# A gated feed-forward kernel: the first stage loads part of x by transposing DMA and its weights through ScalarE's queue

## The chip, the cores and the metric

The kernel runs on one core of one Trainium2 chip. The metric is the device time of one execution in microseconds; the time before is the median of three runs, 558.75 us (558.51 to 558.77). A core has TensorE (PE, matrix multiplies), VectorE (DVE), ScalarE (ACT), GpSimd (POOL) and SyncE (SP, which issues DMAs). Each engine works through its own instructions in order; ScalarE can issue DMAs too, in its own queue. They meet at semaphores.

## What is computed

```
B, S, Dm, Df = 1, 2048, 1024, 3584          # all tensors bf16
g = x @ w_gate                              # [2048, 3584]
u = x @ w_up                                # [2048, 3584]
h = gelu(g) * u                             # tanh form of gelu
out = h @ w_down                            # [2048, 1024]
```

## The kernel before, in words

The 2048 rows of x are done in two passes of 1024 rows, each as two halves of 512 (`xT[0]` and `xT[1]`, held transposed: 128 rows of the contraction on the partitions, eight blocks `ko`, 512 columns). A pass has 14 units (`unit`, L193), one for each 256 columns of `w_gate` and `w_up`, and then `down` (L351) for the product with `w_down`.

A unit computes its 2x2 blocks with seven products in place of eight (Strassen's scheme, in Winograd's form). That needs sums of blocks of x (`t1` to `t4`, L136) and of the weights (`s1` to `s4`, L151), made in fp32r. The x sums are made by VectorE once for a pass. The weight sums are made for each unit: by VectorE for unit 1 of pass 0 and unit 0 of pass 1, by GpSimd for all others (`make_s(ahead, pool)`, L510, one unit ahead). Casts to fp32r (`tb`, `sa`) and copies out of the matmul banks (`snap`) are ScalarE's.

`down` uses the same scheme. For it the raw blocks of `w_down` have to be summed too. In pass 0 GpSimd does that beside the units: `keep(j)` (L258) makes three sums of block j into a tile `m` with one buffer, and `store_made(j)` (L269) writes them to a DRAM tile `td`, from where `load12` (L276) and `load4` fetch them in both passes. Blocks 11, 12 and 13 come in the last unit of pass 0, the last two into spare weight buffers (`w`). SyncE issues all of these DMAs in one written order, among them `fetch12` (L316), which loads the raw halves of `w_down` that `down`'s first product needs (tile `raw`, L319).

The first stage (L417 to L493) stands ahead of the units of pass 0. It does unit 0 without the scheme, in plain bf16 products (`plain`, L451), since sums aren't there yet: for the first 512 rows into banks 0 to 3, then for the second 512 rows into banks 4 to 7. Its weights `wf` come in pieces of `ko`. `w` there (`load_w(1)`, L449) is unit 1's weight tile, w1 below; w2 is the tile after it. x is loaded as it lies in memory (`load_x`, L422, four tiles of 128 rows and 1024 columns) and transposed by TensorE against an identity into a bank, eight 128x128 blocks a tile, and copied from there into `xT` by VectorE or ScalarE (`turn`, L431). Between these stand five warm-up matmuls on zeros, the sums t1, s1, t2, s2, t3, s3, and `finish` (L466): a gelu by ScalarE and a product by VectorE for each of two column blocks.

In the first unit of the schemes (u = 1) `aside(-1)` issues the load of w2 on ScalarE's queue, kept in program order behind the copies `p1` of the first product; `aside(0)` makes s4 and t4 on VectorE. After that `prepare` (L506) has GpSimd make the sums of w2: that is its first work apart from the identity. In pass 0's `down` the x of pass 1 is loaded by transposing DMAs (L553), issued by SyncE between other loads.

The order of SyncE, VectorE, GpSimd and TensorE is the program's (`manual_schedule`), in the first stage ScalarE's too.

Of the kernel before, what the change touches and what calls it, by code (L numbers as in the profile page):

```python
# [10 lines left out]
def kernel(  # L11
# [23 lines left out]
    nc = tc.nc  # L35
    ENG = mybir.EngineType
    ORDER = {ENG.SP, ENG.DVE, ENG.Pool, ENG.PE}
    P = nc.NUM_PARTITIONS
    bf16 = mybir.dt.bfloat16
# [6 lines left out]
    x2 = x.flatten_outer_dims()  # L46
    out2 = out.flatten_outer_dims()
    S, Dm = x2.shape
    Df = w_gate.shape[1]

    NKB = Dm // P
    KH = NKB // 2
    NFB = Df // P
    NJ = NFB // 2
    N = 512
    NS = N // P
# [14 lines left out]
    wpool = ctx.enter_context(tc.tile_pool(name="w", bufs=3))  # L71
# [4 lines left out]
    def new_x():  # L76
        return [xpool.tile([P, NKB, N], bf16, name=f"xT{c}") for c in range(2)]
# [4 lines left out]
    def slot(shape, dtype, name):  # L82
        return kpool.tile(shape, dtype, name=name, tag="k")


    bank = [psum.tile([P, N], f32, name=f"bank{i}") for i in range(8)]
# [23 lines left out]
    def matmul(ps, lhs, rhs, start, stop):  # L110
        nc.tensor.matmul(  # L111
            ps, lhsT=lhs, rhs=rhs, start=start, stop=stop, skip_group_check=True
        )
# [3 lines left out]
    def load_w(u, queue=nc.sync):  # L117
        f0 = u * 2 * P
        w = wpool.tile([P, 2, NKB, 2 * P], bf16, name="w")
        for i, src in enumerate((w_gate, w_up)):  # L120
            got = queue.dma_start(
                out=w[:, i],
                in_=src[:, f0 : f0 + 2 * P].rearrange("(ko ki) f -> ki ko f", ki=P),
            )
            if queue is not nc.sync:
                tc.keep_in_program_order(got)
        return w
# [23 lines left out]
    def sums_s(w, eng):  # L151
        GU = range(2)
        sh = [P, KH, P]
        a11, a21 = [[w[:, i, :KH, h : h + P] for i in GU] for h in (0, P)]
        a12, a22 = [[w[:, i, KH:, h : h + P] for i in GU] for h in (0, P)]
        return Sums(
            how={
                "s1": lambda q: [new(eng, a21[i], a22[i], ADD, "s1", sh) for i in GU],
                "s2": lambda q: [new(eng, q["s1"][i], a11[i], SUB, "s2", sh) for i in GU],
                "s3": lambda q: [new(eng, a11[i], a21[i], SUB, "s3", sh) for i in GU],  # L160
                "s4": lambda q: [new(eng, a12[i], q["s2"][i], SUB, "s4", sh) for i in GU],
                "sa": lambda q: [cast(a22[i], "sa", sh) for i in GU],
            }
        )
# [6 lines left out]
    def make_s(w, eng):  # L171
        s = sums_s(w, eng)
        s.make("s1", "s2", "s3", "sa", "s4")
        return s
# [244 lines left out]
    ident = xpool.tile([P, P], bf16, name="ident")  # L419
    make_identity(nc, ident)  # L420

    def load_x(c):  # L422
        t = []
        for i in range(NS):
            xn = slot([P, Dm], bf16, "xn")
            r0 = c * N + i * P
            nc.sync.dma_start(out=xn, in_=x2[r0 : r0 + P, :])
            t.append(xn)
        return t

    def turn(xT, xn, c, i, copy):  # L431
        tp = bank[4 + i].bitcast(bf16).rearrange("p (k r) -> p k r", k=NKB)
        for ko in range(NKB):
            nc.tensor.transpose(tp[:, ko, :], xn[i][:, ko * P : (ko + 1) * P], ident)
        copy(out=xT[c][:, :, i * P : (i + 1) * P], in_=tp)

    xT = new_x()
    xn0 = load_x(0)
    wf = wpool.tile([P, 2, NKB, 2 * P], bf16, name="w")
    for k0, k1 in ((0, 2), (2, 5), (5, NKB)):  # L440
        for i, src in enumerate((w_gate, w_up)):
            nc.sync.dma_start(
                out=wf[:, i, k0:k1],
                in_=src[k0 * P : k1 * P, 0 : 2 * P].rearrange(
                    "(ko ki) f -> ki ko f", ki=P
                ),
            )
    xn1 = load_x(1)
    w = load_w(1)  # L449

    def plain(ps, c, kos, parts=1):  # L451
        n = N // parts
        for k in range(kos.start, kos.stop, 2):
            for part in range(parts):
                cols = slice(part * n, (part + 1) * n)
                for p, (j, i) in zip(ps, [(j, i) for j in range(2) for i in range(2)]):
                    for ko in (k, k + 1):
                        matmul(
                            p[:, cols],
                            wf[:, i, ko, j * P : (j + 1) * P],  # L460
                            xT[c][:, ko, cols],
                            ko == 0 and part == 0,
                            ko == NKB - 1,
                        )

    def finish(ps, c):  # L466
        for j in range(2):
            times(j, c, gelu(ps[2 * j]), ps[2 * j + 1])

    on_dve, on_act = nc.vector.tensor_copy, nc.scalar.copy  # L470
    s, t = sums_s(w, dve), sums_t(xT)
    with tc.manual_schedule(engines={ENG.Activation}):
        for _ in range(NWARM):
            nc.tensor.matmul(bank[3], lhsT=warm[:, :P], rhs=warm, start=True, stop=True)
        for i in range(NS):
            turn(xT, xn0, 0, i, on_act if i == 1 else on_dve)
        plain(bank[0:4], 0, range(0, 2), parts=2)
        plain(bank[0:4], 0, range(2, 4))
        for i in range(2):
            turn(xT, xn1, 1, i, on_act if i % 2 else on_dve)  # L480
        plain(bank[0:4], 0, range(4, 6))
        for i in range(2, NS):
            turn(xT, xn1, 1, i, on_act if i % 2 else on_dve)
        plain(bank[0:4], 0, range(6, NKB))
        t.make("t1")
        s.make("s1")
        finish(bank[0:4], 0)
        t.make("t2")
        s.make("s2")
        t.make("t3", "tb")  # L490
        s.make("s3", "sa")
        plain(bank[4:8], 1, range(NKB))
        finish(bank[4:8], 1)  # L493

    def making(u):
        if u < 2 or u >= NU:
            return []
        return list(range(u - 2, NJ if u == NU - 1 else u - 1))
# [3 lines left out]
    for ip in range(NPASS):  # L502
        for u in range(1 if ip == 0 else 0, NU):
            js = making(u) if ip == 0 else []

            def prepare():  # L506
                nonlocal ahead
                nxt["w"], nxt["s"] = ahead, None
                if u + 1 < NU:
                    nxt["s"] = make_s(ahead, pool)  # L510
                if u + 2 < NU:
                    ahead = load_w(u + 2)
                if ip == 0:
                    fetch_wd(making(u + 1))
                    for j in making(u - 1):
                        store_made(j)
                for j in js:
                    keep(j, j != js[0])

            def aside(part):  # L520
                nonlocal ahead
                if ahead is None:
                    ahead = load_w(2, nc.scalar)
                if part == 0 and "s4" not in s:
                    s.make("s4")
                    t.make("t4")

            def ahead_of_p4():
                if u + 1 < NU:
                    nxt["p1"] = first_product(even if u % 2 else odd, xT, nxt["w"])  # L530

            e = odd if u % 2 else even
            p1 = nxt.pop("p1", None) or first_product(e, xT, w)
            unit(u, (e, cc, dd), xT, w, s, t, p1, prepare, aside, ahead_of_p4, ip == 0 and u == 1)
            if u + 1 < NU:
                w, s = nxt["w"], nxt["s"]

        last = ip == NPASS - 1
        got, nxt = {}, {}

        def more(step):

            nonlocal ahead
            if last:
                return
            if step == 0:
                xT[:] = new_x()
                for j in making(NU - 1):
                    store_made(j)
            if step >= 16 and step % 2 == 0 and step // 2 - 8 < len(moves):  # L550
                c, ko = moves[step // 2 - 8]
                r0 = (2 * (ip + 1) + c) * N
                nc.sync.dma_start_transpose(  # L553
                    out=xT[c][:, ko, :], in_=x2[r0 : r0 + N, ko * P : (ko + 1) * P]
                )
            if step == 50:
                got["w"], ahead = load_w(0), load_w(1)
            if step == 58:
                got["s"] = make_s(got["w"], dve)
            if step == 62:  # L560
                got["t"] = make_t(xT)

        down(ip, even + cc, dd + odd, last, more)
        even, odd, cc, dd = odd, even, dd, cc
        if not last:
            w, t, s = got["w"], got["t"], got["s"]
# [29 lines left out]
```

## Time and profile before

| what | value |
|---|---|
| median of the runs | 558.75 us (558.51 to 558.77, 3 runs) |
| the profiled execution, its own time | 558.77 us |
| span of the profiled execution (first to last instruction) | 557.0 us |
| TensorE busy | 539.8 us (97%) |
| VectorE busy | 326.2 us (59%) |
| ScalarE busy | 245.4 us (44%) |
| GpSimd busy | 281.3 us (51%) |
| granted TensorE clock, mean | 0.991 |
| DMA | 93.29 MB, 167 GB/s mean |
| first real work of TensorE / begin of unit 1 on TensorE | 3.40 us / 23.16 us |
| first sum of GpSimd for w2 begins / ends | 32.46 us / 35.13 us |

The first stage in the trace, in order of time:

| us | what |
|---|---|
| 0.74 to 2.55 | SyncE issues the four tiles of the first 512 rows of x |
| 2.59 to 5.65 | the six pieces of `wf` |
| 5.69 to 7.60 | the four tiles of the second 512 rows |
| 7.64 to 9.36 | w1, gate and up half |
| 3.40 to 6.42 | TensorE transposes the first rows |
| 6.42 to 10.11 | `plain`, first rows, ko 0 to 3 |
| 10.44 to 14.74 | the rest of it up to ko 5, the transposes of the second rows between |
| 14.74 to 23.16 | `plain`, first rows, ko 6 and 7, then all of the second rows |
| 15.99 to 38 | VectorE works without a break: t1, s1, finish 0, t2, s2, t3, s3, finish 1, then unit 1's sums with s4 (30.42) and t4 (31.62 to 34.11) between |
| 25.31 and 25.77 | ScalarE's queue issues w2, gate and up half |

How to read the profile lines further on: times are microseconds from the span's start. A line of a timeline gives start, duration from the first to the last instruction of the group, engine, source line, operation, output and input by tile name, how many, and in brackets how long the engine was idle before and what released it. SPq and ACTq are the queues in which SyncE and ScalarE issue DMAs; the duration of such a line is that of issuing, not of the transfer. "DMA to landing" is the time from the begin of the issue to the last byte's arrival.

### The profile page before, as it was taken

The numbers are of one execution on the slowest core, as the hardware profiler recorded it, in microseconds if no ns is written. First come the engines' busy times: TensorE is split into PE (matmuls) and PEld (weight loads), VectorE is DVE, ScalarE is ACT, GpSimd is POOL, SyncE is SP. The second block draws the span as 40 slices with busy tenths as digits, with TensorE's granted clock in tenths as the row PEclk, the third lists the DMA queues.
The fourth block names the chain that finished last, engine by engine and source line by source line (L and its number), as shares of the span: only waits on it lengthen the run. The fifth ranks groups of instructions, "written<-read, shape, count | busy, mean of one in ns | idle before, by whom it ended". The sixth has DMA issues, their size and how long they took to land.

```text
span 557.0 us, 7388 instructions
## 1 busy us (share of the span) xinstructions
PE 539.8 (97%) x2437; PEld 380.3 (68%) x2437; DVE 326.2 (59%) x492; ACT 245.4 (44%) x429; POOL 281.3 (51%) x248
## 2 busy tenths in 40 slices
PE   8999999999999939999999999999999999999997
PEld 4577776676677514788877777776766776478886
DVE  2994455545554893469675544555455557856730
ACT  2655554555555201035535555555554552104541
POOL 0069999999999630000049766677777700000000
PEclk9999999999999969999999999999999999999999
DMA  9384676766624579998926233322222049553751
GB/s 277 90 237 114 189 195 186 215 188 182 172 95 171 188 281 324 306 261 231 333 76 154 80 106 106 88 75 76 76 78 75 1 129 381 188 185 118 228 188 58
DMA packets 104359, 93.29 MB, mean 167 GB/s; under 512 B 12929, under 2 KB 88705, under 8 KB 104321
## 3 DMA queue, kind: packets, MB, share of 16 engines
q1 hardware_dynamic: 102240, 91.77, 55.7%
q10 hardware_dynamic: 2080, 1.05, 0.7%
q8 instruction: 20, 0.33, 0.3%
q14 instruction: 19, 0.15, 0.1%
HBM read 75.50 MB, written 15.20 MB: 163 GB/s over the span
## 4 chain that ended last, share of the span: by engine, by line
PE 59%; DMA 4%; POOL 2%; issue 1%; SPq 1%; ACT 0%; POOLq 0%
PE bank L111 59%; DMA raw<-in_w_down_dram 3%; POOL w L93 1%; DMA td<-w 1%; POOL m L93 1%; DMA td<-m 1%; SPq L319 1%; SPq L553 0%; ACT st L398 0%; SPq L280 0%; POOLq L93 0%
## 5 line engine op out<-in xcount | busy, mean ns | idle before, releaser
L93 POOL TENSOR_TENSOR s<-w 128x512 fp32r<-128x512 bf16 x100 | 118.5, 1206 | 157.8 <-DVE t L90 86.8
L111 PE MATMUL bank<-t,s 128*128 128x512 f32 x648 | 157.0, 398 | 0.0
L111 PEld LDWEIGHTS bank<-t,s 128*128 128x128 f32 x648 | 121.8, 188 | 27.7
L107 ACT COPY p<-bank 128x512 f32<-128x512 f32 x124 | 71.3, 589 | 114.3 <-PE bank L111 114.3
L111 PE MATMUL bank<-xT,w 128*128 128x512 bf16 (+1 forms) x504 | 116.6, 377 | 0.0
L90 DVE TENSOR_TENSOR hT<-g,bank 128x512 bf16<-128x512 f32 x112 | 76.7, 687 | 55.0 <-ACT g L178 46.7
L90 DVE TENSOR_TENSOR sum<-bank,p 128x512 f32<-128x512 f32 x54 | 37.3, 691 | 88.4 <-PE bank L111 80.8
L111 PEld LDWEIGHTS <-w 128*128 128x128 bf16 x504 | 45.0, 98 | 58.7 <-issue 13.5
L178 ACT ACTIVATE g<-sum 128x512 f32<-128x512 f32 x81 | 51.3, 633 | 56.6 <-DVE sum L90 55.1
L111 PE MATMUL bank<-raw,hT 128*128 128x512 bf16 x224 | 51.7, 392 | 11.7 <-DMA raw<-in_w_down_dram 11.7
L111 PE MATMUL bank<-q 128*128 128x512 f32 x240 | 59.0, 389 | 0.0
L111 PE MATMUL bank<-t,sa 128*128 128x512 f32 x216 | 58.7, 413 | 0.0
L93 POOL TENSOR_TENSOR s<-w,s 128x512 fp32r<-128x512 bf16 x50 | 57.7, 1177 | 0.0
L93 POOL TENSOR_TENSOR s<-s,w 128x512 fp32r<-128x512 f32 x50 | 57.2, 1166 | 0.0
L111 PE MATMUL bank<-tb,s 128*128 128x512 f32 x216 | 53.3, 389 | 0.0
L111 PEld LDWEIGHTS bank<-q 128*128 128x128 f32 x240 | 45.1, 188 | 9.3
L111 PEld LDWEIGHTS <-hT 128*128 128x128 bf16 x224 | 22.4, 101 | 40.7 <-issue 16.6
L111 PEld LDWEIGHTS bank<-t,sa 128*128 128x128 f32 x216 | 40.7, 188 | 10.6
L111 PEld LDWEIGHTS bank<-tb,s 128*128 128x128 f32 x216 | 40.6, 188 | 8.4
L107 ACT COPY u<-bank 128x512 f32<-128x512 f32 x62 | 35.8, 589 | 23.7 <-PE bank L111 23.3
L102 ACT CAST tb<-raw 128x512 fp32r<-128x512 bf16 x28 | 17.2, 627 | 63.3 <-PE bank L111 27.0
L90 DVE TENSOR_TENSOR q<-hT 128x512 fp32r<-128x512 bf16 x56 | 41.6, 742 | 3.4 <-PE bank L111 3.4
(43 smaller groups left out, 466.9 us busy)
## 6 DMA issues: line engine op xcount, KB each, us to landing
raw<-in_w_down_dram SPq DMA_DIRECT2D x80, 256.0 KB, 3.5
q<-td SPq DMA_DIRECT2D x60, 256.0 KB, 5.0
w<-in_w_gate_dram SPq DMA_DIRECT2D x26, 512.0 KB, 4.2
w<-in_w_up_dram SPq DMA_DIRECT2D x26, 512.0 KB, 5.5
td<-m SPq DMA_DIRECT2D x12, 768.0 KB, 4.5
w<-td SPq DMA_DIRECT2D x6, 1024.0 KB, 8.2
out_dram<-st SPq DMA_DIRECT2D x32, 128.0 KB, 1.7
xn<-in_x_dram SPq DMA_DIRECT2D x8, 256.0 KB, 4.3
```

What stands on the lines that cost most here:

```text
L90: nc.vector.tensor_tensor(out=out, in0=a, in1=b, op=op)
L93: nc.gpsimd.tensor_tensor(out=out, in0=a, in1=b, op=op)
L102: nc.scalar.copy(out=t, in_=src)
L107: nc.scalar.copy(out=t, in_=ps)
L111: nc.tensor.matmul(ps, lhsT=lhs, rhs=rhs, start=start, stop=stop, skip_group_check=True)
L178: nc.scalar.activation(g, src, ACT.Gelu_apprx_tanh)
L319: nc.sync.dma_start(out=rl, in_=wdn[:, kh, j : j + 2, :N])
```

## The change

Only the first stage differs.

- The first 512 rows: columns 0 to 511 (ko 0 to 3) are loaded by four transposing DMAs of 512 rows and 128 columns on SyncE's queue, straight into `xT[0]`. Columns 512 to 1023 are still loaded as they lie (four tiles of 128 x 512) and turned by TensorE, four blocks a tile, into ko 4 to 7.
- The second 512 rows: all eight `ko` by transposing DMAs on SyncE's queue. TensorE and the copying engines have no work on them.
- `wf` (in pieces of ko 0-1, 2-3 and 4-7), the four half-width tiles of x and w1 are issued on ScalarE's queue, in program order.
- TensorE's order: warm-ups, ko 0, ko 1, two tiles turned, ko 2, two tiles turned, ko 3, then ko 4 to 7 in pairs, then the second rows.
- VectorE's order: t1, finish 0, s1, s2, t2, t3, s3, where it was t1, s1, finish 0, t2, s2, t3, s3.
- In `down` the transposing load moves into a helper, with the same instruction.

```diff
-    def load_x(c):
+    def load_x(c, queue):
...
-            xn = slot([P, Dm], bf16, "xn")
+            xn = slot([P, KH * P], bf16, "xn")
...
-            nc.sync.dma_start(out=xn, in_=x2[r0 : r0 + P, :])
+            got = queue.dma_start(out=xn, in_=x2[r0 : r0 + P, KH * P :])
+            tc.keep_in_program_order(got)
...
-        for ko in range(NKB):
+        for ko in range(KH):
             nc.tensor.transpose(tp[:, ko, :], xn[i][:, ko * P : (ko + 1) * P], ident)
-        copy(out=xT[c][:, :, i * P : (i + 1) * P], in_=tp)
+        copy(out=xT[c][:, KH:, i * P : (i + 1) * P], in_=tp[:, :KH])
+
+    def transposing(xT, c, ko, r0):
+        nc.sync.dma_start_transpose(
+            out=xT[c][:, ko, :], in_=x2[r0 : r0 + N, ko * P : (ko + 1) * P]
+        )
...
-    for k0, k1 in ((0, 2), (2, 5), (5, NKB)):
+    for ko in range(KH):
+        transposing(xT, 0, ko, 0)
+    load_wf(nc.scalar, 0, 2)
+    load_wf(nc.scalar, 2, 4)
+    xn0 = load_x(0, nc.scalar)
+    load_wf(nc.scalar, 4, NKB)
+    for ko in range(NKB):
+        transposing(xT, 1, ko, N)
+    w = load_w(1, nc.scalar)
...
-        for i in range(NS):
-            turn(xT, xn0, 0, i, on_act if i == 1 else on_dve)
-        plain(bank[0:4], 0, range(0, 2), parts=2)
-        plain(bank[0:4], 0, range(2, 4))
+        plain(bank[0:4], 0, range(0, 1))
+        plain(bank[0:4], 0, range(1, 2))
         for i in range(2):
-            turn(xT, xn1, 1, i, on_act if i % 2 else on_dve)
-        plain(bank[0:4], 0, range(4, 6))
+            turn(xT, xn0, 0, i, on_act if i % 2 else on_dve)
+        plain(bank[0:4], 0, range(2, 3))
         for i in range(2, NS):
-            turn(xT, xn1, 1, i, on_act if i % 2 else on_dve)
-        plain(bank[0:4], 0, range(6, NKB))
+            turn(xT, xn0, 0, i, on_act if i % 2 else on_dve)
+        plain(bank[0:4], 0, range(3, 4))
+        plain(bank[0:4], 0, range(4, NKB))
         t.make("t1")
-        s.make("s1")
         finish(bank[0:4], 0)
-        t.make("t2")
-        s.make("s2")
-        t.make("t3", "tb")
+        s.make("s1", "s2")
+        t.make("t2", "t3", "tb")
         s.make("s3", "sa")
         plain(bank[4:8], 1, range(NKB))
         finish(bank[4:8], 1)
```

`load_wf(queue, k0, k1)` issues the gate and the up piece of `wf` on the given queue; the loop that it replaces issued the same on SyncE's.

## The prediction

> **What bounds the kernel now.** I read the page's busy rows first, then the chain of waits, then GpSimd's and TensorE's timelines, then the first 36 us engine by engine. The busy rows of the page (tenths of 40 slices, 13.9 us each):
>
> ```profile
> PE   8999999999999939999999999999999999999997
> POOL 0069999999999630000049766677777700000000
> PEclk9999999999999969999999999999999999999999
> ```
>
> TensorE (PE) looks like the bound everywhere, but slice 14 has a hole (a 3, with the granted clock down), and GpSimd (POOL) is full from slice 3 up to just before that hole. The chain of waits says what filled it (start, duration, what):
>
> ```profile
> 181.66 4.45 issue
> ...
> 196.43 1.49 POOL w L93
> ...
> 199.50 4.32 DMA td<-w
> ...
> 204.92 2.39 SPq L319
> ...
> 224.37 329.45 PE bank L111 x1464
> ```
>
> Followed back, the end of the kernel hangs on GpSimd's last down-weight sum (199.50). SyncE's queue holds the store of those sums behind them, and behind that store it holds the reloads at L319 that feed the first down product. So TensorE waited here (start, duration, group, idle before it):
>
> ```profile
> 204.57 6.01 PE L111 MATMUL bank<-raw,hT 128*128 128x512 bf16 x16 [10.36 <-DMA raw<-in_w_down_dram]
> ```
>
> 10.36 us of TensorE's time in pass 0 are slack: if TensorE alone comes earlier or some microseconds later there, nothing at the end moves. What moves the end is when GpSimd begins, as its timeline shows:
>
> ```profile
> 32.46 3.79 POOL L93 TENSOR_TENSOR s<-w 128x512 fp32r<-128x512 bf16 x2 [31.16 <-DMA w<-in_w_gate_dram]
> 36.20 2.30 POOL L93 TENSOR_TENSOR s<-s,w 128x512 fp32r<-128x512 f32 x2
> ...
> 179.24 2.43 POOL L93 TENSOR_TENSOR m<-raw,m 128x512 fp32r<-128x512 bf16 x2
> 186.12 1.16 POOL L93 TENSOR_TENSOR m<-raw 128x512 fp32r<-128x512 bf16 x1 [4.46 <-issue]
> ```
>
> From 36.20 to 181.67 it has no gap at all; the one gap, 4.46 us, is the store of the single buffer m. So whatever shifts the first pair (32.46) shifts the kernel's end by as much. That pair takes 3.79 us where later pairs take 2.3: its first sum runs 2.67 us, to 35.13. VectorE's (DVE) timeline gives the reason:
>
> ```profile
> 30.42 1.28 DVE L90 TENSOR_TENSOR s<-w,s 128x512 fp32r<-128x512 bf16 x2
> 31.62 2.49 DVE L90 TENSOR_TENSOR t<-xT,t 128x512 fp32r<-128x512 bf16 x4
> 34.03 0.68 DVE L90 TENSOR_TENSOR hT<-g,bank 128x512 bf16<-128x512 f32 x1
> ```
>
> The four t4 sums end at 34.11, GpSimd's first 1.02 us later. At the start of pass 1 it is the same: VectorE's t sums end at 289.22, GpSimd's first, begun at 286.28, ends at 290.24, again 1.02 later. GpSimd stands still while VectorE runs back-to-back sums on two SBUF operands. So GpSimd's first sum ends at the later of (landing of w2's gate half plus about 1.1) and (end of t4 plus 1.02); the second sum needs the up half, landed by 34.21, where it could start at 35.09: 0.88 us to spare.
>
> **The change, part by part.** Call T0 to T11 the twelve transposing loads, all on SyncE: T0 to T3 fill xT0's ko 0 to 3, T4 to T11 xT1's ko 0 to 7.
>
> Removed on TensorE: 48 of 64 transposes. Eight take 0.45 us of weight loads (0.056 each at full rate): 48 are 2.7 us. Removed on VectorE and ScalarE: four of eight xT copies, the others halved; they had covers and cost no path. Bytes stay as they were: 8 x 256 KB of x and 2 MB of weights, 4.2 MB, which the first 16 us carried at 317 to 330 GB/s.
>
> Added on SyncE:
>
> ```profile
> L553 SPq DMA_TRANSPOSE xT<-in_x_dram x16: 1122/1138/2318, 212.0 to 253.0; - x16
> DMA to landing us min/median/max: 2.9/4.3/7.5
> ```
>
> Three of them back to back took 3.73 us with their gaps, so a pitch of 1.17 to 1.3 (the first of all took 2.32, with the queue full). I take 1.17: T_k is issued at 0.74 + 1.17k. T0 lands alone, 2.9 to 3.4 later: 4.0. In the loaded stretch I take 6.6, the landing of the second and third of pass 0, issued under a full queue (bounds 2.9 and 7.5): T7 lands at 0.74 + 8.2 + 6.6 = 15.5 (12 to 16.5). T11, when the rest is through, 4.3: 17.9 (16.5 to 21).
>
> A rule speaks against this: the Trainium skill, "VectorE: DVE Perf Modes", Rules for kernel authors, would give a 128x128 transpose to TensorE wherever PSUM will do as its target, and The three transpose paths puts it at 1309 ns by DMA against 390 by TensorE. One after the other 48 blocks would be an estimated 63 us by that page and the kernel some 45 us slower; the rows above, four blocks in 1.14 us of issue, overrule it.
>
> Moved to ScalarE (ACT): twelve loads (four of wf, four of half-width xn0, two of wf, two of w1), from 0.73 on. Issues on that queue cost 0.42 and 0.59 in the trace, so 6.4 us end it at best. But a queue with much outstanding holds its issuer: on SyncE w1's second half took 0.88 at 8.48, and the third and fourth of four such loads in a row 2.90 and 1.61 (260.9 to 265.5). I take 8.7 (6.4 to 9.5). Behind it wait ScalarE's table load (1.28, which ran at 0.73 in the idle start before) and its two xT copies, some 0.6 each (half of 1.01, plus its fixed part): done at 11.2 (9 to 12).
>
> TensorE then: ko 0 at 4.0, ko 1 with T1 (4.8) to 5.9, transposes of xn0 rows 0 and 1 (landed about 6.7), ko 2 (0.86), transposes 2 and 3 (about 8.1), ko 3 to 9.4; ko 4 to 7 wait for ScalarE's second copy, 11.2, and take 16 x 0.216 = 3.5: 14.7. Second rows 32 x 0.216 = 6.9: unit 1 begins at 21.6 against 23.16 (at 26.62 the first product with t follows 16 matmuls of 0.216). Without the hold it is 20.2, limited by transposes and landings; T11 needs no more than 17.9 + 0.9. The clock may stay halved for some microseconds more, since TensorE idles between warm-up and ko 0; the first eight matmuls would cost 1.7 us more, under the arrival of T2 and the copies.
>
> VectorE's order becomes t1, products of finish 0, s1, s2, t2, t3, s3, products of finish 1, s4, t4. t1 ends with T7: 15.5 + 0.7 = 16.2; the two products 17.4 (gelu is done by 15.0); w1, the last of 4.2 MB, has landed by then: 1.8 (first bytes) + 13.7 + 0.7. From s1 to finish 1 are 14 sums at 0.602: 8.4, so 25.8 against 28.03, 2.2 us earlier, and t4 ends at 31.9 (30.7 to 34). No stall of TensorE interferes: it supplies finish 1 by 22.
>
> GpSimd: w2 is issued behind unit 1's first copies, 2.15 after its begin: 23.75; its halves land 7.1 and 8.4 later as now: 30.9 and 32.6. That falls into the s4 and t4 run, so GpSimd's first sum ends at 31.9 + 1.02 = 32.9 against 35.13: **2.2 us earlier**, all of which reaches the end. Sum: profiled run 558.77 (span 557.0 and 1.77 around it; the median of the runs is 558.75) less 2.2 gives **556.6 us**. Its own range: t4 at 30.7 and unit 1 at 20.2 give 3.4 less, 555.3; t4 at 33 gives 557.6.
>
> **Rivals.** First, no gain: ScalarE's queue is served behind SyncE's. For it: w2, issued at 25.31, lies behind loads of SyncE, and from 25.4 to 28.4 only SyncE's queue moved bytes; the other came after 28.5. Then w1 lands after T11, near 19.6, s1 starts when it would have had to start anyway (18.40 and the 1.2 of the products now put ahead), and t4 ends at 34: 558.7. Against it: at a pitch of 1.17 the transposes leave the engines half free. The Trainium skill, "DMA: Bandwidth & Descriptors", Queues, rings and completion order, says that each DMA engine takes packets of the queues in turn; by that w1 would not wait and the estimate stays 556.6.
>
> Second, slower: both queues' issues pass one after the other, and the pitch of T grows. T11 at 0.74 + 11p + 4.3 decides when unit 1 begins (0.9 later). Up to T11 = 23.2, p = 1.65, GpSimd's 0.88 us of slack on the up half still covers it; above, each 0.1 of p costs 1.1 us. Twelve loads of 0.5 among twelve transposes of 1.2 make p = 1.7 (559.4); at 1.9 it is 561.5; at the 2.32 of the first one 566. For it: that 2.32, and landings of 6.6 to 7.5 under load. Against: three in a row under a busy queue kept 1.17 to 1.3.
>
> Third, more gain than I count: T7 lands by 13.5, ScalarE isn't held and unit 1 starts before 20: 555.
>
> **How the numbers follow.** Forecast (555.3 to 557.6) 0.58, more gain 0.04, no gain 0.20, slower 0.18. Within 0.2% of 558.75 is 557.6 to 559.9, about what a measurement of this kernel tells from no change. The no-gain case lies there; of the slower case 0.02 stays inside. Faster 0.62, same 0.22, slower 0.16. The range 555.2 to 559.8 leaves out some 0.04 below and 0.16 above.
>
> **What would show it.** GpSimd's first sum should end near 32.9 and right behind t4's end, its last near 197.3, and TensorE's wait before L319's data be about 9.7. The transposing loads should stand 1.17 to 1.3 apart and the twelfth land by 18; ScalarE's last first-stage issue should end near 8.7 and ko 4 start near 11. I am wrong if GpSimd pauses between 36 and 181, if the pitch is above 1.6, or if w1 lands after 19.

## The result and the profile after

| | before | after |
|---|---|---|
| median of the runs | 558.76 us (558.51 to 560.13, 4 runs) | 564.71 us (563.92 to 565.12, 4 runs) |
| span of the profiled execution | 557.0 us | 562.9 us |
| unit 1's first product with t on TensorE begins | 26.64 us | 33.98 us |
| t4 ends on VectorE | 34.11 us | 39.33 us |
| GpSimd's first sum ends / its third begins | 35.13 / 36.20 us | 41.08 / 42.82 us |
| GpSimd's last sum of pass 0 ends | 199.48 us | 205.77 us |

The changed kernel is slower: ratio 1.0100, 95% interval 1.0080 to 1.0119. The forecast was 556.6 us, faster, with a range of 555.2 to 559.8; the time lies 4.9 us above that range.

The end still hangs where it did. The chain of waits of the changed kernel (start, duration, what):

```profile
188.23 4.48 issue
...
204.27 1.50 POOL w L93
...
205.79 4.31 DMA td<-w
...
221.62 338.07 PE bank L111 x1504
```

GpSimd's (POOL) last down-weight sum, the store behind it, a reload of `raw`, and then TensorE to the end: the same links as before, each some 6 us later. (Before, TensorE waited once more, 0.23 us at 224.37, so its last piece is counted from there; the group that starts here at 221.62 started at 215.34.) TensorE's timeline, at the place where it had 10.36 us to spare:

```profile
210.84 5.30 PE L111 MATMUL bank<-raw,hT 128*128 128x512 bf16 x16 [9.29 <-DMA raw<-in_w_down_dram]
```

It still waits 9.29 us there. So TensorE's delay costs nothing at this place; what costs is that GpSimd began late. GpSimd's timeline, and VectorE's (DVE) beside it:

```profile
39.91 1.17 POOL L93 TENSOR_TENSOR s<-w 128x512 fp32r<-128x512 bf16 x1 [38.60 <-DMA w<-in_w_gate_dram]
41.71 1.16 POOL L93 TENSOR_TENSOR s<-w 128x512 fp32r<-128x512 bf16 x1 [0.64 <-DMA w<-in_w_up_dram]
42.82 2.30 POOL L93 TENSOR_TENSOR s<-s,w 128x512 fp32r<-128x512 f32 x2
```

```profile
36.84 2.49 DVE L90 TENSOR_TENSOR t<-xT,t 128x512 fp32r<-128x512 bf16 x4
39.25 0.68 DVE L90 TENSOR_TENSOR hT<-g,bank 128x512 bf16<-128x512 f32 x1
```

t4 is over before GpSimd's first sum begins, which now takes 1.17 us and not 2.67: nothing blocks it any more. It waits for w2, and w2 is issued by ScalarE behind unit 1's first product, 7.3 us later than before. The up half of w2 lands 7.45 us later (41.64 against 34.19); before, it had 0.88 us to spare, now the second sum waits for it, so the third sum begins 6.62 us later. From there to the end the kernel takes 0.7 us less than before, which no run explains; that leaves the 5.9 us of the span.

Why unit 1 is late is read in ScalarE's (ACT) timeline; ACTq lines are its DMA issues:

```profile
4.94 2.32 ACTq L427 DMA_DIRECT2D xn<-in_x_dram  x4
8.62 0.42 ACTq L445 DMA_DIRECT2D w<-in_w_gate_dram  x1
13.58 0.39 ACTq L445 DMA_DIRECT2D w<-in_w_up_dram  x1
14.01 0.52 ACTq L121 DMA_DIRECT2D w<-in_w_gate_dram  x1
14.57 0.65 ACTq L121 DMA_DIRECT2D w<-in_w_up_dram  x1
15.26 1.28 ACT L436 ACT_TABLE_LOAD   x1 [15.26 <-issue]
16.55 1.07 ACT L436 COPY xT<-bank 128x512 bf16<-128x512 bf16 x2
```

The issues take 0.35 to 0.65 us each, but there are holes of 2.20, 1.36 and 4.54 us before 4.94, 8.62 and 13.58. The program explains them, and the trace records which semaphore each DMA signals and which one its issue waits for: every DMA of both queues signals one of eight completion semaphores, given out in turn over both queues, and an issue waits until the DMA that had the same semaphore before has landed. The trace has these landings:

| issue on ScalarE's queue | at | the DMA that had its semaphore | landed |
|---|---|---|---|
| xn, first tile | 4.94 | T0, issued by SyncE at 0.74 | 4.92 |
| wf, ko 4 to 7, gate | 8.62 | xn, first tile | 8.60 |
| wf, ko 4 to 7, up | 13.58 | T6, issued by SyncE at 8.52 | 13.56 |
| w1, gate | 14.01 | T7, issued by SyncE at 9.83 | 13.99 |

So in three of the four, and in 6.7 of the 8.1 us of holes, ScalarE waits in its own issues for SyncE's transposing loads; the other one, at 8.62, waits for a plain load of its own queue. Behind these issues stand its table load and the two copies that ko 4 needs, and TensorE's timeline ends the story:

```profile
11.43 1.03 PE L111 MATMUL bank<-xT,w 128*128 128x512 bf16 x4
17.68 16.66 PE L111 MATMUL bank<-xT,w 128*128 128x512 bf16 x64 [5.21 <-ACT xT L436]
33.98 5.82 PE L111 MATMUL bank<-t,s 128*128 128x512 f32 x24
```

It stands still for 5.21 us, and then half its clock is gone. The stretches before and behind 17.6 us (the columns: stretch, its length, PE busy, granted clock, DMA share, GB/s):

```profile
12.50:17.60 5.10, 0.00 (x0) 0.87 1.01 201
17.60:23.10 5.50, 5.42 (x13) 0.50 0.80 166
```

13 matmuls in 5.42 us are 0.42 each, where 0.216 is the full rate. A last line asks for more than waits: what the DMA engines carried on both queues together from 1.8 to 11 us (the DMA view of that stretch, kernel after).

```profile
DMA packets 4977, 1.86 MB, mean 202 GB/s; under 512 B 3392, under 2 KB 4977, under 8 KB 4977
```

In the same 9.2 us the kernel before moved 2.92 MB at 318 GB/s, in 3164 packets. Now it is a third less, in more and smaller packets, with the engines shown as busy throughout (a DMA share of 0.99 to 1.26 from 3 to 13 us). Three suspects, then: the waits of one queue for the other, the transposing loads themselves, and the two queues side by side.

### The profile page after: what moved, and what is told of

It reads as the page before. It is cut to its first block, busy times and chain, and to the rows that moved or that the text cites. A ratio compares the mean times of both kernels' runs of the same rounds, so it can differ in the third digit from the quotient of the medians.

```text
span 562.9 us, 7271 instructions
## 1 busy us (share of the span) xinstructions
PE 540.0 (96%) x2381; PEld 377.2 (67%) x2381; DVE 324.1 (58%) x489; ACT 243.9 (43%) x428; POOL 279.5 (50%) x248
## 3 DMA queue, kind: packets, MB, share of 16 engines
q10 hardware_dynamic: 6880, 3.67, 2.8%
## 4 chain that ended last, share of the span: by engine, by line
PE 60%; DMA 3%; POOL 1%; issue 1%; ACT 0%; SPq 0%; POOLq 0%
PE bank L111 60%; DMA raw<-in_w_down_dram 2%; POOL w L93 1%; DMA td<-w 1%; POOL m L93 1%; DMA td<-m 1%; ACT st L398 0%; SPq L280 0%; POOLq L93 0%
## 5 line engine op out<-in xcount | busy, mean ns | idle before, releaser
L93 POOL TENSOR_TENSOR s<-w 128x512 fp32r<-128x512 bf16 x100 | 116.8, 1187 | 165.5 <-DVE t L90 86.4
L111 PE MATMUL bank<-xT,w 128*128 128x512 bf16 x496 | 121.0, 391 | 6.7 <-ACT xT L436 5.2
L111 PE MATMUL bank<-raw,hT 128*128 128x512 bf16 x224 | 50.9, 388 | 11.2 <-DMA raw<-in_w_down_dram 11.2
```

The source lines that it names most:

```text
L93: nc.gpsimd.tensor_tensor(out=out, in0=a, in1=b, op=op)
L111: nc.tensor.matmul(ps, lhsT=lhs, rhs=rhs, start=start, stop=stop, skip_group_check=True)
```

## The experiments

All in one table first. The ratio is to the kernel before, run on the same chip, with its 95% interval; e1 and e2 are single runs. The last three columns are of the profiled execution, whose own time can lie up to 1.7 us off the median (e3: 560.79, e10: 558.38): begin of unit 1's first product with t, begin of GpSimd's third sum, and how long after that the span ended.

| run | median us | ratio | t product | third sum | rest of the span |
|---|---|---|---|---|---|
| before | 558.76 | | 26.64 | 36.20 | 520.8 |
| after | 564.71 | 1.0080 to 1.0119 | 33.98 | 42.82 | 520.1 |
| e1 copies on VectorE | 563.78 | | 32.27 | 41.23 | 520.8 |
| e2 w1 on SyncE | 561.85 | | 31.15 | 39.89 | 520.1 |
| e3 fewer, larger loads | 562.32 | 1.0043 to 1.0081 | 29.69 | 38.59 | 520.4 |
| e4 w2 early | 562.07 | 1.0039 to 1.0079 | 26.74 | 29.20 | 530.8 |
| e5 straight loads | 560.37 | 1.0007 to 1.0046 | 29.43 | 38.34 | 520.2 |
| e6 filler matmuls | 562.37 | 1.0054 to 1.0099 | 31.27 | 40.05 | 520.1 |
| e7 second rows only | 566.59 | 1.0120 to 1.0156 | 28.35 | 34.51 | 530.0 |
| e8 weights on ScalarE | 563.17 | 1.0068 to 1.0098 | 31.52 | 41.09 | 520.7 |
| e9 gate half first | 560.53 | 1.0019 to 1.0043 | 27.35 | 38.25 | 520.8 |
| e10 gate half, w2 early | 556.70 | 0.9952 to 0.9975 | 27.96 | 35.92 | 520.5 |
| e11 straight, copies on VectorE | 557.28 | 0.9960 to 0.9984 | 26.52 | 35.28 | 520.1 |
| e12 mended change | 560.76 | 1.0022 to 1.0047 | 30.03 | 38.98 | 521.0 |

In twelve of fourteen rows the rest of the span is 520.1 to 521.0 us, while the third sum's begin moves over 7.5 us: the time of this kernel is read off the moment when GpSimd has its first pair of sums done. The two exceptions are taken up below.

**e1: are ScalarE's two copies the cause?** The changed kernel with all four copies on VectorE.

```diff
-            turn(xT, xn0, 0, i, on_act if i % 2 else on_dve)
+            turn(xT, xn0, 0, i, on_dve)
```

> The changed kernel with all four copies of turned x on VectorE instead of two on ScalarE. In the changed kernel the second rows' first matmul group (ko 4 on) began at 17.68, behind ScalarE's table load and two copies, which came behind its last DMA issue (15.22). Theory S (an issue on ScalarE's queue waits until the DMA that had the same semaphore before it, mostly a transposing load, has landed): ScalarE's issues stay where they were (4.94, 8.62, 13.58); the copies are done by 12, but the up piece of ko 4 to 7, issued at 13.58, lands only near 16.9, so ko 4 begins at 16.9 and the time falls by about 0.7 us to 564.0. Theory C (only the two copies behind the queue are late, the data are there): ko 4 begins near 11, TensorE's clock does not fall, and the time falls by 7 us or more to 557.

Measured: 563.78 us. TensorE's timeline:

```profile
13.43 0.60 PE L111 MATMUL bank<-xT,w 128*128 128x512 bf16 x2 [0.47 <-DMA w<-in_w_gate_dram]
17.39 15.24 PE L111 MATMUL bank<-xT,w 128*128 128x512 bf16 x60 [3.35 <-DMA w<-in_w_up_dram]
```

The copies no longer hold ko 4, but its weights do: their up half is issued at 13.61 and lands near 17. The late issues have two victims, and sparing one leaves the other, as theory S said.

**e2: is it what is outstanding on ScalarE's own queue?** w1, the megabyte at its end, goes to SyncE behind T11.

```diff
-    w = load_w(1, nc.scalar)
+    w = load_w(1)
```

> The changed kernel with the two loads of w1 (1 MB) back on SyncE's queue, behind the twelfth transposing load. Theory R (my prediction's: ScalarE's queue is held because much data is outstanding on it): with 1 MB less the last issue of the first stage ends by 7, the copies are done by 10, ko 4 begins near 11 and the time is 557 to 559. Theory S (waits for semaphores of transposing loads): the four tiles of x are issued from 4.9, the gate piece of ko 4 to 7 at 8.6 and the up piece at 13.6 as in the changed kernel; the copies come about 1.2 us earlier, but that piece lands near 16.9, so ko 4 begins at 16.9: 563.5 to 564.5.

Measured: 561.85 us. ScalarE's timeline begins its first work with

```profile
13.14 1.28 ACT L436 ACT_TABLE_LOAD   x1 [13.14 <-DMA xT<-in_x_dram]
```

With w1 off its queue ScalarE is still held until 13.1, and the line names what it waited for: a transposing load (T6, landed at 12.70; the issue behind it stands at 12.72). "Held by outstanding data", which the prediction had assumed, falls. The time came out 1.6 below what the other theory had said.

**e3: the waits for transposing loads taken away** by fewer and larger loads, so that ScalarE issues all of `wf` before a semaphore comes round again, and none of its issues takes over a transposing load's semaphore. xn goes to SyncE behind T0.

```diff
+    transposing(xT, 0, 0, 0)
+    xn0 = load_x(0, nc.sync)
+    for ko in range(1, KH):
...
-    load_wf(nc.scalar, 2, 4)
-    xn0 = load_x(0, nc.scalar)
-    load_wf(nc.scalar, 4, NKB)
+    load_wf(nc.scalar, 2, NKB)
+    w = load_w(1, nc.scalar)
```

> The changed kernel with the same bytes in fewer DMAs, ordered so that no load on ScalarE's queue takes over a transposing load's semaphore: wf in pieces of ko 0-1 and 2-7, x's turned half in two DMAs on SyncE's queue behind the first transposing load. The transposing loads and w1 on ScalarE's queue stay. Theory S: ScalarE's last issue ends before 10, ko 4 begins at 11 to 12, no fall of TensorE's clock, unit 1 begins near 22 and the time is 556.5 to 558.5. Theory T (the transposing loads themselves, at a pitch of 1.30 and landing 4 to 7 us after issue, cost the time): ko 4 and the second rows stay late, 562 or more.

Measured: 562.32 us. ScalarE is free sooner, as meant (table load at 11.03), yet only 4.3 of the 7.3 us came back. (Two holes stay in ScalarE's issues, up to 7.98 and 10.61: they end with the landing of a tile of xn and of a piece of `wf`, plain loads both.) T1, issued at 3.14, landed at 10.93, 7.8 us later, behind what both queues had in flight, and TensorE waited 4.61 us for it before ko 1. The waits for transposing loads are a part of the loss; the late arrival of what TensorE needs is another. The second isn't shown here to be the transposing loads' own: xn and the large pieces of `wf`, issued just before T1, took 5.9 to 8.3 us too.

**e5 and e11: the same change with straight loads.** In e5 the twelve transposing loads are plain ones of as many bytes (128 rows by 512 columns). Both kernels leave out the transposition of these blocks, so they don't compute the product; only their time counts.

```diff
-        transposing(xT, 0, ko, 0)
+        straight(xT, 0, ko, 0)
...
-        transposing(xT, 1, ko, N)
+        straight(xT, 1, ko, N)
```

> The changed kernel with the twelve transposing loads of the first stage replaced by plain loads of as many bytes (128 rows of x by 512 columns, straight into the same tiles), on the same queue, in the same place and with the same semaphores; what is computed from those tiles is therefore not the reference's. Nothing else differs. Theory T (the transposing loads are the root: their landing, 4 to 7 us, is what ScalarE's issues wait for, and they slow what the other queue carries): plain loads land within 2.5 us, the waits for shared semaphores shrink, ScalarE's last issue is out by 9, TensorE takes ko 4 by 12.5, the first product of unit 1 runs by 22.5, time 555.5 to 558.5. Theory Q (ScalarE's queue is what is slow: two queues filled at once hold each other up, whatever the loads on the other are): ScalarE's last issue stays behind 12, time 561 or more.

e11 is e5 with the edit of e1 added.

> e5_straight_copies (plain loads in place of the transposing ones) with all four copies of the turned blocks on VectorE as well, so that nothing of what TensorE waits for stands behind ScalarE's issues. Theory A (what is left of the loss in e5, 2.8 us at unit 1's first t,s product, is the two copies that ScalarE makes after its last issue and its table load, and the half clock after the idle 2.2 us): ko 4 starts by 13.2, the clock stays full, the t,s product starts at 26.0 to 27.2, time 558.0 to 559.2. Theory B (it is the sharing of the engines by two queues, weights and x at once): ko 4 waits for its weights until 14 or later, the t,s product stays at 28.5 or later, time 560 or more.

Measured: 560.37 us (557.84 to 561.30) and 557.28 us. In e5 ScalarE's issues end at 12.0 and not at 15.2, and 276 GB/s move from 1.8 to 11 us; ko 4 begins at 14.47, behind ScalarE's table load and copies. That lies between the two theories. In e11 nothing of that is left:

```profile
12.56 0.60 PE L111 MATMUL bank<-xT,w 128*128 128x512 bf16 x2 [0.41 <-DMA w<-in_w_gate_dram]
13.31 13.56 PE L111 MATMUL bank<-xT,w 128*128 128x512 bf16 x62 [0.15 <-DMA w<-in_w_up_dram]
26.52 5.84 PE L111 MATMUL bank<-t,s 128*128 128x512 f32 x24
```

ko 4 runs at 12.56, the clock stays full, and the kernel is 1.5 us faster than before, though ScalarE's issues still end only at 11.9: nothing that TensorE needs stands behind them. Theory A fits, up to its time, which is 0.7 too long. So, taken in this order and from one execution each, the 7.34 us of unit 1 split as follows: 4.55 (33.98 to 29.43) go with the transposing loads, 2.91 (29.43 to 26.52) with ScalarE's copies standing behind its issues and the half clock that follows, and what remains is -0.12. The order of the copies alone, with the transposing loads kept, is worth 1.71 (e1). One of e5's five executions took 557.84 us at a mean clock of 0.993, the others 560.3 and more at 0.987 or 0.988, which suggests that the second term isn't the same every time.

**e6: the price of the clock.** 24 matmuls on zeros fill TensorE's idle 5.2 us.

```diff
+        for _ in range(24):
+            nc.tensor.matmul(bank[4], lhsT=warm[:, :P], rhs=warm, start=True, stop=True)
         plain(bank[0:4], 0, range(4, NKB))
```

> The changed kernel with 24 more matmuls of the zero tile into a bank that is free, put on TensorE between ko 3 and ko 4, where it otherwise stands idle for 5.2 us. They compute nothing that is used. Theory K (the idle time has a second price, the half clock at which ko 4 to 7 then run, 13 matmuls in 5.42 us): the granted clock stays full from 12.5 on, ko 4 to 7 take 3.5 instead of 6.0 us, the first product of unit 1 comes 2.5 earlier, time 561.7 to 562.7. Theory L (the late landing of the second rows' last transposing load, or VectorE's sums, hold unit 0's second half anyway): the clock is full but unit 1 comes less than 0.8 earlier, time 563.8 to 565.

Measured: 562.37 us, unit 1's product at 31.27. The same two stretches as above, of this kernel:

```profile
12.50:17.60 5.10, 5.10 (x25) 1.00 0.90 162
17.60:23.10 5.50, 5.50 (x27) 1.00 1.01 199
```

The same 5.5 us hold twice the matmuls. As theory K said, the half clock cost 2.71 us at unit 1's product and 2.77 at GpSimd's third sum; the median fell by 2.3.

**e12: the change, mended where it can be.** e1, e2 and 14 filler matmuls together, the transposing loads kept.

```diff
-            turn(xT, xn0, 0, i, on_act if i % 2 else on_dve)
+            turn(xT, xn0, 0, i, on_dve)
...
-    w = load_w(1, nc.scalar)
+    w = load_w(1)
...
+        for _ in range(14):
+            nc.tensor.matmul(bank[4], lhsT=warm[:, :P], rhs=warm, start=True, stop=True)
```

> The changed kernel with three things mended at once and its transposing loads kept: all four copies on VectorE, unit 1's weights on SyncE behind the last transposing load, and 14 matmuls of the zero tile between ko 3 and ko 4 to keep TensorE's clock. Theory S (the waits for shared semaphores, the copies and the clock are separate terms; the transposing loads themselves leave a remainder): ScalarE's last issue at 12.7 and its landing at 15.5 hold ko 4, which then runs at full clock, the t,s product starts at 29.2 to 30.2, time 560.2 to 561.5. Theory Z (mended in these three, the change is worth what it takes off TensorE): the t,s product before 27, time 558.5 or less.

Measured: 560.76 us, the product at 30.03. That is theory S. Two thirds of the loss are gone; with the transposing loads kept, 3.5 us against e11 at the product and 2 us against the kernel before at the end remain.

**e7 and e8: each half of the change alone.** e7 puts the second rows' transposing loads on SyncE, behind the first weights, and leaves the rest as before.

```diff
-    xn1 = load_x(1)
+    for ko in range(NKB):
+        nc.sync.dma_start_transpose(
+            out=xT[1][:, ko, :], in_=x2[N : 2 * N, ko * P : (ko + 1) * P]
+        )
     w = load_w(1)
...
-        for i in range(2):
-            turn(xT, xn1, 1, i, on_act if i % 2 else on_dve)
...
-        for i in range(2, NS):
-            turn(xT, xn1, 1, i, on_act if i % 2 else on_dve)
```

> The kernel before with one part of the change: the second rows of x come by eight transposing loads instead of four plain loads, 32 transposes on TensorE and four copies; they stay on SyncE's queue, behind the first weights and ahead of unit 1's weights, and the first rows and all weights are loaded as before. Theory W (the loss is the wait of one queue's issues for the other's transposing loads; on a queue of their own the loads are worth the 32 transposes, 2.5 us of TensorE): each transposing load waits only for plain loads, T7 lands by 20.5, unit 1's first product runs at 21.5 to 23, GpSimd's first sum ends by 35.5, time 556.5 to 559.0. Theory T (a transposing load costs more than the transposes it saves wherever it stands: issues at a pitch of 1.3 or more, landings of 4 to 7 us, lower throughput of what is loaded beside it, here unit 1's weights): unit 1's first product comes after 24.5, time 560 or more.

e8 moves the weights alone to ScalarE's queue.

```diff
-            nc.sync.dma_start(
+            got = nc.scalar.dma_start(
...
-    w = load_w(1)
+    w = load_w(1, nc.scalar)
...
-            turn(xT, xn0, 0, i, on_act if i == 1 else on_dve)
+            turn(xT, xn0, 0, i, on_dve)
```

> The kernel before with the other part of the change alone: the first weights and unit 1's weights are issued by ScalarE instead of SyncE, x stays on SyncE and is turned by TensorE; the copy of the first rows that ScalarE made goes to VectorE, since ScalarE is busy with issues then. Theory W or T (without transposing loads the waits for shared semaphores are waits for plain loads, 2 to 3 us, and two queues together carry as much as one): ScalarE's last issue is out by 10, unit 1's first product within 1.5 us of before's 23.16, time 557.5 to 560.0. Theory Q (two queues filled at once hold each other up): throughput of the first 11 us under 260 GB/s against 318 in the kernel before, unit 1's first product after 26, time 561 or more.

Measured: 566.59 and 563.17 us; both halves lose by themselves. For e7 theory T gives product and time (its landings are 2.7 to 4.5 us and not 4 to 7): the eight issues take 11.39 us, 1.42 each (one of them 2.25), so w1 is issued only at 17.12 and lands at 21.51 and 23.28; VectorE stands still for 8.45 us before it. In e8 neither theory fits whole. Two queues carry as much as one (317 GB/s from 1.8 to 11 us, where theory Q had less than 260), yet x comes late: the fourth tile is issued at 4.11 and not at 2.12, since its semaphore was that of a weight piece that landed at 4.09, and it lands 5.53 us later where it took 3.80 before. TensorE's timeline:

```profile
9.69 1.03 PE L434 MATMUL bank<-ident,xn 128*128 128x128 bf16 x8 [3.07 <-DMA xn<-in_x_dram]
```

One queue in the order of need had x first. On two, weights and x share the engines and the semaphores, and what is needed first is no longer first.

**e4, e9 and e10: what lets GpSimd begin.** These start from the kernel before. e4 loads w2 as early as can be:

```diff
+    w2 = load_w(2)
...
-                    ahead = load_w(2, nc.scalar)
+                    ahead = w2
```

> The kernel before, with w2's load issued on SyncE's queue right behind w1's (near 9.5) instead of on ScalarE's at 25.31. Tests that the end hangs on the begin of GpSimd's sums. If only w2's landing held GpSimd, it begins near 17.5 and the end comes about 10 us earlier (until TensorE's own wait of 10.36 us is used up): 548 to 550. If VectorE's back-to-back sums on two SBUF operands hold it too, GpSimd gets in only where VectorE works from the matmul banks (19.6 and 28.0 to 30.4) until 34.1: two to four sums done by then, 1.1 us each: 554.5 to 556.5. If the end did not hang on GpSimd: 558.7.

Measured: 562.07 us. GpSimd's and VectorE's timelines:

```profile
19.74 1.17 POOL L93 TENSOR_TENSOR s<-w 128x512 fp32r<-128x512 bf16 x1 [18.44 <-DMA w<-in_w_gate_dram]
21.21 8.02 POOL L93 TENSOR_TENSOR s<-w 128x512 fp32r<-128x512 bf16 x1 [0.30 <-DMA w<-in_w_up_dram]
```

```profile
30.52 3.10 DVE L90 TENSOR_TENSOR s<-w,s 128x512 fp32r<-128x512 bf16 x2
33.54 6.34 DVE L90 TENSOR_TENSOR t<-xT,t 128x512 fp32r<-128x512 bf16 x4
```

GpSimd begins 13 us earlier and loses: its second sum takes 8.02 us under VectorE's back-to-back sums, then the two alternate, t4 takes 6.34 us where it took 2.49, and TensorE waits 4.47 us for it. Later GpSimd waits 1.83 us for VectorE and 2.82, 0.67 and 2.95 us for stores of m (up to 64.83, 78.15 and 182.09), waits that the kernel before doesn't have; the store at 59.56 stands on SyncE's queue right behind two loads of `raw`. None of the expected figures came. This is the first exception of the table. e7 is the second, for the same reason: w2 landed there in the midst of VectorE's late sums, t4 took 6.34 us as well, and the same three waits for m followed (2.98, 0.65 and 3.10 us).

e9 loads the gate half of w1 ahead of the second rows and has VectorE make that half's sums while it would wait.

```diff
+    load_half(0, w_gate)
     xn1 = load_x(1)
-    w = load_w(1)
+    load_half(1, w_up)
...
+        half(0, True)
...
+        half(0, False)
```

> The kernel before, with no part of the change: the gate half of unit 1's weights is loaded ahead of the second rows of x and the up half behind them, and VectorE makes the gate half's four sums while it would wait, so that t4 ends earlier. It asks for the step of the prediction that GpSimd's start follows the end of t4. Theory G (that step): t4 ends at 31.5 to 32.5 against 34.11, GpSimd's second sum ends 1 to 2 us earlier than 36.25, time 556.7 to 557.9. Theory W2 (GpSimd's start is set by the landing of unit 2's weights, issued by ScalarE after unit 1's first product, 7 us before they land): t4 ends earlier, GpSimd's first sum still starts at 32.4 or later, its second ends within 0.9 of 36.25 plus the delay of unit 1, time 558.0 to 559.5.

Measured: 560.53 us. t4 ends at 32.54, as meant, and GpSimd's timeline shows what that is worth:

```profile
33.52 1.16 POOL L93 TENSOR_TENSOR s<-w 128x512 fp32r<-128x512 bf16 x1 [32.22 <-DMA w<-in_w_gate_dram]
37.13 1.16 POOL L93 TENSOR_TENSOR s<-w 128x512 fp32r<-128x512 bf16 x1 [2.44 <-DMA w<-in_w_up_dram]
```

Nothing: it waits for w2, and longer for the up half than before, since a load of SyncE into the buffer of w1, which had waited for s4, now came at 27.78 and not at 31.86, into w2's transfer. Theory W2 is right in kind and too low in size.

e10 adds to e9 the early w2, and one GpSimd copy of a column of t4 that keeps its sums out of VectorE's.

```diff
+    w2 = load_w(2)
...
                     t.make("t4")
+                    nc.gpsimd.tensor_copy(out=tiny, in_=t["t4"][KH - 1][:, :1])
```

> e9_gate_half_first with unit 2's weights loaded by SyncE right behind unit 1's, and one more GpSimd instruction ahead of its first sum, a copy of one column of t4, which holds its start until VectorE's sums are done (in e4_w2_early it started among them, and both were slowed). Theory G: GpSimd's first sum starts at t4's end, 31.5 to 32.5, second sum ends by 35.0, time 556.0 to 557.4. Theory H (an earlier start of GpSimd is not worth its size, since later its sums wait for TensorE through the weights' buffers and for the store of the down-weight sums): the second sum ends by 35.0 and yet the time is 558 or more.

Measured: 556.70 us (556.26 to 558.38, 7 runs), faster than both kernels, ratio 0.9964 (0.9952 to 0.9975). GpSimd's timeline:

```profile
33.53 0.18 POOL L547 CAST tiny<-t 128x1 fp32r<-128x1 f32 x1 [32.23 <-DVE t L90]
33.67 2.28 POOL L93 TENSOR_TENSOR s<-w 128x512 fp32r<-128x512 bf16 x2
```

Its first pair runs unhindered right behind t4. The profiled execution is the longest of the seven (558.38 us), and t4 ended there at 33.5, later than was said, and GpSimd's second sum at 35.95; the median is within theory G's figure. e10 has nothing of the change in it.

## Why the prediction was wrong

- **GpSimd's chain sets the end, TensorE has slack in pass 0: right.** Twelve rows of the table keep 520.1 to 521.0 us from GpSimd's third sum to the end, and TensorE still waits 9.29 us in pass 0. That this is near the 9.7 foreseen is luck: TensorE came 7.3 us later there and its data 6.3, where the prediction had both earlier.
- **ScalarE's queue is held by outstanding data, last issue done at 8.7 (6.4 to 9.5), and with it the two copies at 11.2 (9 to 12): the step that failed.** The issue was done at 15.2, the copies at 17.6. The 0.88 to 2.90 us issues that I read as "held" gave a wrong mechanism and so a wrong bound: no issue of ScalarE took over 0.65 us here. What holds an issue is the landing of the DMA that last had its semaphore, and the semaphores go round over both queues: by moving the weights to another queue the change made ScalarE wait for SyncE's transposing loads. e2 shows it, and so do the four issue times that stand 0.02 us behind landings. From ScalarE's delay followed ko 4 at 17.68 and not 11.2, VectorE's 8.19 us of standing still before finish 0's first product (23.06), which the prediction had ruled out ("no stall of TensorE interferes"), and w1 landed at 19.31 and 22.42, the prediction's own sign of being wrong (after 19). It isn't the whole loss: with the waits for transposing loads taken away, 4.3 of 7.3 us came back (e3).
- **The transposing loads: the pitch was nearly right (1.30 for 1.17) and T7 landed at 14.0, before the 15.5 foreseen.** T0 and T1 came later than foreseen (4.92 and 6.73 for 4.0 and 4.8). But I charged them only to the matmuls and sums that read them. Their landing of 4.2 to 5.0 us (T0 to T7) entered three of ScalarE's four waits, and both queues together carried a mean of 202 GB/s, where I had kept 317 to 330: that term of the sum was mis-sized, too. Straight loads give back 4.55 us at unit 1's product; the 45 us that the prediction worked out for the blocks one after the other, and set aside, didn't come either.
- **The half clock: foreseen at the first eight matmuls, under cover; it came there (3.67 us for the eight) and once more at ko 4 to 7, on the path.** The second time it cost 2.71 us (e6).
- **VectorE's chain and GpSimd's block: right wherever the loads let it be seen.** e11 has t4 end at 31.94 (31.9 foreseen) and lands at 557.28, inside the forecast's own range of 555.3 to 557.6. But GpSimd isn't blocked there any more and waits for w2's up half, landed at 34.1 and not at 32.6: its third sum begins 0.9 us earlier than before, and the other 0.7 of the 1.6 us of the span lie behind it. So that the time falls into the range is in part luck.
- **The rival "slower" had the right sign and the wrong mechanism.** It let the pitch grow to 1.7 or more; the pitch stayed at 1.30, and T11, landed at 22.6 (17.9 foreseen), held nothing up. The loss went through ScalarE. The rival "no gain" had w1 land late, and it did, but because it was issued only at 14.01 and 14.57.

The rule of the semaphores could have been read before the change. The chain of waits of the kernel before has it on SyncE's queue: a load of `raw` lands at 216.81, and that lets a transposing load of x be issued which takes over its semaphore.

```profile
207.41 9.40 DMA raw<-in_w_down_dram
...
216.82 1.12 SPq L553
```

Left open: how much of the 4.55 us is the landing of a transposing load and how much the lower throughput beside it; no run separates them. Nor is it shown that the transposition itself is the cause: the transposing loads also come in smaller pieces (3392 of 4977 packets under 512 B from 1.8 to 11 us, 286 of 3574 in e5), and plain loads in pieces as small were not run.

## What to carry to other kernels

Before moving loads to another engine's queue, list which completion semaphore each DMA gets: an issue waits for the DMA that had it before, on whatever queue that was, and with it everything behind it on the issuing engine. Put nothing that another engine needs soon behind DMA issues (e5 against e11), and see that what is needed first isn't issued after, or beside, what is needed later (e8). Find the one event that sets the end, here GpSimd's first pair of sums, and count a gain only where it moves that event; an earlier start amid VectorE's sums was worth less than nothing (e4) until it was held back to their end (e10).

## What the hardware showed beyond expectation

- Transposing loads lower what the engines carry in all: 202 GB/s over 9.2 us against 276 with straight loads in their place and 317 for two queues of plain loads, at a busy share of 0.9 to 1.1. With nothing else in flight (e7, 12.5 to 17.6 us) they moved 90 GB/s at a share of 0.57, about one load of 128 KB in each 1.42 us of issue. The Trainium skill, "Advanced Engine Details and Errata", X-Bar Transpose (TRN2), says that transposing DMAs are as fast as regular ones; for blocks of 512 x 128 in bf16 the rows here differ, at an issue every 1.30 to 1.42 us for 128 KB.
- VectorE and GpSimd starve each other over many instructions: one sum of GpSimd took 8.02 us and not 1.16, and four of VectorE 6.34 and not 2.49. The Trainium skill, "SBUF — State Buffer", SBUF: two separate sides, has the port pair locked by the op that starts first, for the whole instruction; the 8.02 us are longer than any one VectorE op (0.69), so there the loser didn't get in between the next ones. The sum ended at 29.23, 1.03 us after the last of VectorE's sums s3 (28.20).
- TensorE's clock fell to half after idle times as short as 1.5 us (e5: idle from 12.3, half from 13.8) and stayed there for 3.4 us (e1, e2, e5) or 6.8 us (after, e8). How much idle time it takes no run isolates: in e5 shorter gaps lay before it.
